# Attention, gated layer and softplus layer in one kernel: x left undivided by its rms in the first layer, and another form of the first batch's softmax

## The chip, the cores and the metric

The kernel runs on one core of a Trainium2 chip. The metric is device time in microseconds (us). TensorE does the matrix products into eight PSUM banks; VectorE and ScalarE read these banks and work on SBUF; GpSimd helps VectorE with work in SBUF; SyncE issues the transfers between HBM and SBUF. Each engine runs its own list of instructions in order and waits at semaphores for the others.

## The reference

Three stages run one after the other on 4 batches of 576 tokens.

```
scores = q @ k.T / 8           # 8 heads of 64; heads 0-3 local: the 32 latest keys,
                               # heads 4-7 strided: keys at the same position modulo 32
attn = exp(scores - max); attn = attn / (sum(attn) + 1e-9)
x = (attn @ v), laid out as 2304 tokens x 512
xn = x / sqrt(mean(x * x) + 1e-6) * rms_g          # one rms for each token
x = (silu(xn @ w_gate) * (xn @ w_val)) @ w_out     # 512 -> 1536 -> 512
h = x @ w_in; x = softplus(h) @ w_out2             # 512 -> 2048 -> 512
```

## The kernel before, in words

**Layout.** x stands turned, features on partitions, as four tiles of 128 features (kk = 0 to 3). The 2304 tokens are cut in chunks c of 512 (the last of 256). Side A is chunks 0 and 1 (side index 0), side B is chunks 2, 3 and 4. A float32 product is made of halves: each operand is split into a high half and a low half, and `mm3` (L434) issues three matmuls for each product. Splitting x takes a ScalarE copy (L351, tile `ob`) and a subtraction (L355 when it is on VectorE, L356 on GpSimd). Weights come in packed words, and `decode` (L370 to L376) unpacks them with one ScalarE and three VectorE instructions before they are split into `win` or `wout`.

**Attention.** A unit is one batch, one pair of heads and one half of its blocks. Local pairs have blocks of 64 queries and 96 keys, 5 and 4 of them in the two units; strided pairs have blocks of 54, 6 and 5 of them. Units 0 to 15 are batches 0 and 1 and run in `attend`, as the startup of the program; units 16 to 31 are put between the first layer's work by `steps`. A unit goes: mask and scores on TensorE (L553, L566), maximum on VectorE (L581), exponentials on ScalarE, sums and division (L610, L611, `stage_p`), transposes of the probabilities (L637), their eviction to `pt`, product with v (L660), eviction to `xs`. For units 0 to 15 the exponentials are one instruction for each block, straight from the bank and with the row's sum as a second result (L599); for units from 16 on VectorE subtracts the maximum first (L583), one ScalarE instruction does the whole unit (L596), and VectorE adds up (L609).

**Statistics and the first layer.** `stats(c)` squares the chunk on ScalarE (L452), sums over features by four matmuls with ones (L453), takes a logarithm and an exponential (L457, L458) and three VectorE steps (L459 to L462); `norm` then multiplies x by the result and by rms_g (L472), and only then is x split. `half(f, c)` makes the gate and value products of block f of 128 hidden features for chunk c; Gate and value banks of side A come from one ring of two. `chain1` takes silu of the gate bank (L867), multiplies by the value bank (L868) and splits (L856 and `gl` on L355); `out1` is the product with w_out, added into x by L899 and L901. The startup does blocks 0 and 1 for chunk 0, then `stats(1)` between two loads of ScalarE's function table, then `half(0, 1)`. After that `side_a` goes through the blocks for both chunks, with queued steps of attention in between. `gv` is a ring of buffers for chain1; the `ssq` rows of chunks 0 and 1 join it once these chunks are divided.

**Order.** Engine calls are recorded as nodes with a cost and their reads and writes (`Program.add`). `emit` plans the nodes of a whole section: it gives each a due time, tries several orders against a model of the engines (with LEAVE, SWITCH and the costs of DMAs), picks for some nodes VectorE or ScalarE, or VectorE or GpSimd (`evict`, `two`), and issues the best order found. So a change of a cost or of a dependency can move instructions anywhere in the section. One section runs from the start to block 9 of side A, a second one covers the rest.

Of the kernel before, what the change touches and what calls it, by code (L numbers as in the profile page):

```python
# [49 lines left out]
WINDOW = 3413  # L50
TURNS, KEEP, SWITCH, LEAVE = 8, 0.5, 125, 4000

# [195 lines left out]
def attn_glu_softplus(  # L248
# [16 lines left out]
    def all_of(key):  # L265
        return (key, 0, 1 << 30)
# [81 lines left out]
    def split_op(src, ksrc, slot, k, n0=0, eng="POOL"):  # L348
# [11 lines left out]

    hold = []

    def decode(src, t, kt, keep):

        raw, kraw = raws.next()
        u, ku = cvu.next()
        words = raw.bitcast(U32).rearrange("p (n two) -> p n two", two=2)
        wlo, whi = words[:, :, 0], words[:, :, 1]
        dma(512, lambda: nc.sync.dma_start(out=raw, in_=src), hold, [kraw])
# [9 lines left out]
        dma(256, lambda: nc.sync.dma_start(out=wk[keep], in_=t), [kt], [("wk", keep, keep + 1)])  # L379

# [59 lines left out]
    def stats(c, ring_):  # L440
# [37 lines left out]
    def attention(at, use):  # L478

        def whole(u):  # L480
            return u >= 16

        qks = ring(at, "qk", 3, [128, 2 * QW])
        mask = at.tile([128, MW], BF16, name="mask")
        dma(100, lambda: nc.sync.dma_start(out=mask, in_=masks), [], [all_of("mask")])
        vb = ring(at, "vb", 2, [128, 9, 128])
        eb = ring(at, "eb", EB, [128, 5 * LK])
        pp = ring(at, "pp", 2, [128, 6, 128])
        pt = ring(at, "pt", 4, [128, 3 * 128])
        sq = ring(at, "sq", 2, [128, 6 * SK])  # L490
        mz = ring(at, "mz", 8, [128, 2, 6])
# [41 lines left out]
        def stage_s(u):  # L533
# [48 lines left out]
            if whole(u):  # L582
                dve(n * nk, lambda: nc.vector.tensor_sub(ev, sv, m.unsqueeze(2).to_broadcast([128, n, nk])),  # L583
                    [kb_, km], [ke])
            else:
                dve(6, lambda: nc.vector.tensor_scalar(out=m, in0=m, scalar1=-SCALE, scalar2=None, op0=ALU.mult),
                    [km], [km])
            scored[u] = (e, ke, ev, z, kz, sv, kb_, m, km)

        def stage_e(u):  # L590
            b, p, t0, n = units[u]
            loc = p < 2
            nk = LK if loc else SK
            e, ke, ev, z, kz, sv, kb_, m, km = scored.pop(u)
            if whole(u):
# [28 lines left out]
        def stage_t(u):  # L624
# [8 lines left out]
            for a0 in range(0, n, 3):  # L633
                m = min(n, a0 + 3) - a0
                tp, ktp = use.t.next()
                for a in range(m):
                    pr.add("PE", 108, lambda a=a, a0=a0, tp=tp: nc.tensor.transpose(  # L637
                        tp[:kp, a * 128:a * 128 + 128], pv[:, a0 + a, :], id_sb), [kpv, all_of("id")], [ktp])
                t, kt = pt.next()
                evict(2 * m * nq, t[:kp, :2 * m * nq].rearrange("p (m c) -> p m c", c=nq),  # L640
                      tp[:kp, :m * 128].rearrange("p (m c) -> p m c", c=64)[:, :, :nq], [ktp], [kt])
                res.append((t, kt))
            trans[u] = res
            if p >= 2:
                trans[u - 1] = res

        def stage_v(u):
# [8 lines left out]
            for a in range(n):  # L656
                t, kt = pts[a // 3]
                for h in range(2):
                    o = (2 * (a % 3) + (h ^ (u % 2))) * nq
                    pr.add("PE", 59, lambda a=a, h=h, o=o, t=t: nc.tensor.matmul(  # L660
                        xb[64 * h:64 * h + 64, a * nq:(a + 1) * nq], lhsT=vt[r0:r1, v0 + a, 64 * h:64 * h + 64],
                        rhs=t[r0:r1, o:o + nq], start=True, stop=True), [all_of(kv), kt],
                        [kx], mode=1 if loc else 3)
            g = rg_sb[:, p:p + 1]
            if loc:
# [70 lines left out]
    def steps(at, after, ring_):  # L736
# [3 lines left out]
        def turn(us, cs):  # L740
# [118 lines left out]

    def chain1(gate, val, n=CH, r4=False, eng="POOL"):  # L860
# [117 lines left out]
    with tc.manual_schedule():  # L978
# [56 lines left out]
        def side_a(f, queue):  # L1035
# [4 lines left out]
            for c in (0, 1) if f > 1 else (1,):  # L1040
# [12 lines left out]
        with ExitStack() as c2:  # L1053
# [7 lines left out]
            for f in (0, 1):  # L1061
                g[f, 0] = chain1(*gates.pop((f, 0)))
            o_banks.t = f_banks.t
# [13 lines left out]
            for i in (0, 1):  # L1077
                fk["gv"].keys[len(fk["gv"].t)] = ("ssq", i * CH, i * CH + CH)
# [139 lines left out]
```

## Time and profile before

| what | value |
|---|---|
| time, median of three runs | 901.63 us (901.39 to 902.55) |
| the profiled execution | 900.52 us, span 898.7 us, mean granted clock 0.993 |
| TensorE busy | 882.7 us, 98% of the span |
| VectorE busy | 712.9 us, 79% |
| ScalarE busy | 486.1 us, 54% |
| GpSimd busy | 28.1 us, 26 instructions |
| share of the chain that ended last | TensorE 67%, VectorE 3% |

A busy time is what the engine's rows cover, and a matmul's row runs a little past the start of the next one; shares over the whole span mix a startup, in which the engines wait for each other, with hundreds of microseconds in which TensorE never stops.

### The profile page before, as it was taken

How to read it: one execution, taken by the hardware profiler on the slowest of the kernel's cores; microseconds unless marked ns; L12 is line 12 of the kernel's file. 1: busy time of each engine (PE TensorE's matmuls, PEld its weight loads, DVE VectorE, ACT ScalarE, POOL GpSimd, SP SyncE). 2: the span in 40 equal slices, each digit the busy share in tenths (PEclk: the TensorE clock that was granted, in tenths of full speed). 3: DMA queues.
4: the chain of work that ended last, by engine and by line, in shares of the span. 5: the costliest groups of instructions: out<-in, count | busy, mean ns of one | idle time of the engine just before them, and what ended most of it. 6: DMA issues, size and time to landing. Idle time of an engine off the chain costs nothing.

```text
span 898.7 us, 14075 instructions
## 1 busy us (share of the span) xinstructions
PE 882.7 (98%) x5320; PEld 725.7 (81%) x5320; DVE 712.9 (79%) x1349; ACT 486.1 (54%) x999; POOL 28.1 (3%) x26
## 2 busy tenths in 40 slices
PE   7899999999999999999999999999999999999998
PEld 6567777778777888888888888888888888888886
DVE  4988898998599995888988799877798456676644
ACT  5987664545364675444545567544474655434331
POOL 0000010200000000000100100000000000000000
PEclk7999999999999999999999999999999999999999
DMA  7874667363040443344553025321114111111003
GB/s 254 263 228 146 205 205 224 124 214 106 13 141 23 151 152 105 134 146 140 183 154 104 2 85 178 137 71 48 47 47 153 36 47 48 47 32 39 1 1 117
DMA packets 41858, 102.18 MB, mean 114 GB/s; under 512 B 4800, under 2 KB 5568, under 8 KB 41792
## 3 DMA queue, kind: packets, MB, share of 16 engines
q1 hardware_dynamic: 41792, 101.31, 35.5%
q8 instruction: 41, 0.67, 0.3%
q14 instruction: 25, 0.20, 0.1%
HBM read 78.74 MB, written 22.54 MB: 113 GB/s over the span
## 4 chain that ended last, share of the span: by engine, by line
PE 67%; DVE 3%; issue 0%
PE bank L434 67%; DVE xs L901 1%; DVE ob L355 0%; DVE tb L355 0%; DVE xs L355 0%; DVE win L355 0%; DVE w L355 0%; DVE ssq L355 0%; DVE glx L355 0%; DVE xs L919 0%; DVE gv L355 0%; DVE ssq L868 0%; DVE gv L868 0%; DVE gl L355 0%
## 5 line engine op out<-in xcount | busy, mean ns | idle before, releaser
L434 PE MATMUL bank<-ob,win 128*128 128x512 f32 (+1 forms) x1560 | 430.8, 360 | 2.7 <-ACT ob L351 1.8
L434 PEld LDWEIGHTS bank<-ob,win 128*128 128x128 f32 x1560 | 283.4, 188 | 55.0 <-ACT ob L351 2.2
L434 PE MATMUL bank<-tb,win 128*128 128x512 f32 x672 | 232.8, 392 | 0.0
L434 PEld LDWEIGHTS bank<-tb,win 128*128 128x128 f32 x672 | 125.4, 188 | 22.9 <-DVE xs L901 0.4
L919 DVE TENSOR_TENSOR xs<-bank,xs 128x512 f32<-128x512 f32 x126 | 86.8, 689 | 45.7 <-PE bank L434 44.4
L405 ACT ACTIVATE win<-w 128x512 fp32r<-128x512 f32 (+1 forms) x136 | 83.4, 616 | 63.9 <-PE bank L434 32.7
L355 DVE TENSOR_TENSOR win<-w,win 128x512 fp32r<-128x512 f32 (+1 forms) x134 | 89.5, 673 | 15.6 <-ACT win L405 12.6
L434 PE MATMUL bank<-wout,ghx 128*128 128x512 f32 x304 | 100.0, 390 | 0.0
L434 PE MATMUL bank<-wout,gh 128*128 128x512 f32 x272 | 90.4, 390 | 0.0
L434 PE MATMUL bank<-ghx,wout 128*128 128x512 f32 x224 | 84.1, 394 | 0.0
L434 PE MATMUL bank<-gh,wout 128*128 128x512 f32 (+1 forms) x256 | 81.3, 356 | 0.5 <-DVE xs L901 0.4
L901 DVE TENSOR_TENSOR xs<-bank,xs 128x512 f32<-128x512 f32 (+1 forms) x100 | 62.2, 628 | 8.9 <-PE bank L434 8.1
L434 PEld LDWEIGHTS bank<-wout,ghx 128*128 128x128 f32 x304 | 56.9, 188 | 11.7
L434 PEld LDWEIGHTS bank<-wout,gh 128*128 128x128 f32 x272 | 50.9, 188 | 10.6
L816 ACT ACTIVATE gv<-bank 128x512 f32<-128x512 f32 x48 | 28.4, 592 | 48.1 <-PE bank L434 47.6
L434 PE MATMUL bank<-wout,glx 128*128 128x512 f32 x152 | 53.2, 389 | 0.0
L434 PEld LDWEIGHTS bank<-gh,wout 128*128 128x128 f32 x256 | 45.5, 189 | 9.0 <-DVE xs L901 1.4
L434 PEld LDWEIGHTS bank<-ghx,wout 128*128 128x128 f32 x224 | 41.9, 188 | 8.4 <-ACT ghx L856 0.2
L434 PE MATMUL bank<-wout,gl 128*128 128x512 f32 x136 | 47.7, 389 | 0.0
L373 DVE SCALAR_TENSOR_TENSOR cvu<-raw,cvu 128x512 uint32<-128x512 uint32 x68 | 46.6, 686 | 1.0
L355 DVE TENSOR_TENSOR w<-w 128x256 f32<-128x256 f32 x109 | 45.4, 416 | 0.9
L820 DVE TENSOR_TENSOR gv<-bank,gv 128x512 f32<-128x512 f32 x48 | 32.9, 685 | 16.0 <-ACT gv L816 9.0
(131 smaller groups left out, 1211.8 us busy)
## 6 DMA issues: line engine op xcount, KB each, us to landing
raw<-w SPq DMA_DIRECT2D x68, 512.0 KB, 4.1
w<-w_kept SPq DMA_DIRECT2D x56, 256.0 KB, 2.6
w_kept<-cvtx SPq DMA_DIRECT2D x26, 256.0 KB, 3.7
cvt<-w_kept SPq DMA_DIRECT2D x26, 256.0 KB, 2.7
w_kept<-w SPq DMA_DIRECT2D x24, 256.0 KB, 4.2
qk<-qk SPq DMA_DIRECT2D x8, 601.0 KB, 5.6
w_kept<-cvt SPq DMA_DIRECT2D x18, 256.0 KB, 3.5
cvtx<-w_kept SPq DMA_DIRECT2D x18, 256.0 KB, 2.8
```

Of the source, the lines that this page charges most:

```text
L355: pr.add("DVE", 68 + n / 0.96, lambda: getattr(nc.vector, name)(o, x, y), r, w, alt=(110 + n * 2.3, lambda: getattr(nc.gpsimd, name)(o, x, ...
L373: dve(512, lambda: nc.vector.scalar_tensor_tensor(out=u, in0=wlo, scalar=29, in1=u, op0=ALU.logical_shift_right, op1=ALU.bitwise_or), [kra ...
L405: act(n, lambda: nc.scalar.activation(h, t, AF.Copy), [kt], [reg(0, o + lo, o + hi)])
L434: lambda a=a, b=b, i=i, st=st, mv=mv: nc.tensor.matmul(o, lhsT=st[a], rhs=mv[b], start=(first and i == 0), stop=(last and i == m - 1), ski ...
L816: act(CH, lambda: nc.scalar.activation(o, y[0], AF.Copy), [y[1]], [ko])
L820: dve(CH, lambda: nc.vector.tensor_add(o[0], y[0], o[0]), [y[1], o[1]], [o[1]])
L901: dve(n, lambda: nc.vector.tensor_add(x, pb, x), [kp, kx], [kx])
L919: dve(DM, lambda: nc.vector.tensor_add(x, pb, x), [kp, kx], [kx])
```

## The change

1. **Undivided x for side A** (`RAW`). x of chunks 0 and 1 is no longer multiplied by the statistics before it is split: `raw_op` splits x times rms_g (ScalarE copy with a scale, VectorE scalar_tensor_tensor). In `chain1` VectorE multiplies the gate bank by the statistics (new line L932) before silu, which now reads SBUF. The value product stays undivided, and at the end of side A x of chunks 0 and 1 is multiplied by the statistics once (eight `xs<-xs,ssq` pieces). As `ssq` is then needed all through side A, two new tiles `gvx` take its place in the ring of `gv`, and for blocks 10 and 11 the ring has two buffers.
2. **Statistics.** `stats(0)` is recorded after `half(0, 0)`. `stats(1)` loses its own pair of table loads: it runs in the first turn of `steps`, and five steps of the queue are recorded right after `half(0, 1)`.
3. **Batch 0's strided units** (2, 3, 6 and 7) use the form that units from 16 on have: subtraction, one exponential for the unit, sum on VectorE.
4. **Batch 0's first local pair** (units 0 and 1, `late`): VectorE subtracts, TensorE transposes the scores, and the exponential is the eviction of the transposed tile (L670). The product with v is turned round (queries on partitions) with a column of ones in v that gives the sums; VectorE divides (L685 to L689), and 18 small identity matmuls (L695) turn the result back.
5. **Planner numbers**: LEAVE 4000 to 6000, and other costs for some DMAs. v's tiles are 130 wide, not 128.

```diff
+RAW = (0, 1)
-TURNS, KEEP, SWITCH, LEAVE = 8, 0.5, 125, 4000
+TURNS, KEEP, SWITCH, LEAVE = 8, 0.5, 125, 6000
...
+    def raw_op(src, ksrc, slot, k, kk):
+        (h, l), (kh, kl) = op_of(slot, k)
+        g, kg = rg_sb[:, kk:kk + 1], all_of("rg")
+        act(CH, lambda: nc.scalar.activation(h, src, AF.Copy, scale=g), [ksrc, kg], [kh])
+        pr.add("DVE", 130 + CH / 0.96, lambda: nc.vector.scalar_tensor_tensor(
+            out=l, in0=src, scalar=g, in1=h.bitcast(F32), op0=ALU.mult, op1=ALU.subtract), [ksrc, kh, kg], [kl])
...
-        if c < 2:
+        if c < 2 and c not in RAW:
             norm(c, "DVE")
...
         def whole(u):
-            return u >= 16
+            return u >= 16 or u in (2,3,6,7)
+
+        def late(u):
+            return u in (0,1)
...
             else:
+                pv, kpv = ev, ke
...
+                dve(n * nk, lambda: nc.vector.tensor_sub(
+                    pv[:, :, :nk], sv, m.unsqueeze(2).to_broadcast([128, n, nk])), [kb_, km], [kpv])
...
+                if late(u):
+                    act(m * 128, lambda t=t, tp=tp, m=m: nc.scalar.activation(
+                        t[:kp, :m * 128], tp[:kp, :m * 128], AF.Exp, scale=SCALE), [ktp], [kt], True)
...
+        def turned(xb, kx, n, nq):
...
+            dve(6, lambda: nc.vector.tensor_scalar_add(out=z, in0=xv[:, :, 64], scalar1=1e-9), [kx], [kz])
+            dve(30, lambda: nc.vector.reciprocal(out=z, in_=z), [kz], [kz])
...
+            dve(n * 64, lambda: nc.vector.tensor_mul(
+                y, xv[:, :, :64], z.unsqueeze(2).to_broadcast([128, n, 64])), [kx, kz], [ky])
...
+                    pr.add("PE", 47, lambda a=a, r=r, i=i: nc.tensor.matmul(
+                        xt[r, a * nq:(a + 1) * nq], lhsT=y[i, a, :], rhs=id_sb[i, i], start=True, stop=True),
+                        [ky, all_of("id")], [kt], mode=3)
...
             for c in cs:
-                norm(c, "POOL")
+                if c > 1:
+                    norm(c, "POOL")
...
+        if c in RAW:
+            r, kr = sview(CUTS[c], CUTS[c + 1]), ("ssq", CUTS[c], CUTS[c + 1])
+            dve(n, lambda a=a, gb=gb: nc.vector.tensor_mul(a, gb, r), [kg, kr], [ka])
+            gb, kg = a, ka
         act(n, lambda: nc.scalar.activation(a, gb, AF.Silu), [kg], [ka], True)
...
         def early():
             use.s = s_banks
-            stats(0, f_banks)
             direct(0)
             half(0, 0, f_banks)
+            stats(0, v_banks)
...
-            table(EXP_LN)
-            stats(1, t_banks)
-            table("silu_and_others")
             direct(1)
             half(0, 1, v_banks)
...
-            queue, last_turn = steps(x, {1: (2,)}, tv)
+            queue, last_turn = steps(x, {-1: (1,), 1: (2,)}, tv)
+            step(queue, 5)
...
+        for c in RAW:
+            for kk in range(KD):
+                x, kx = xv(kk, c)
+                two("POOL", CH, "tensor_mul", x, x, sview(CUTS[c], CUTS[c + 1]), [kx, ("ssq", CUTS[c], CUTS[c + 1])], [kx])
+        give(RAW)
```

What stands on the engines is shown at three places. First ScalarE at the program's start, where `eb` is a unit's buffer of scores or probabilities. Before, from its first exponential on:

```order
L599 ACTIVATE eb_116,mz_129<-bank_71,mz_129 128x96
L599 ACTIVATE eb_115,mz_128<-bank_70,mz_128 128x96
L599 ACTIVATE eb_116,mz_129<-bank_71,mz_129 128x96
L599 ACTIVATE eb_115,mz_128<-bank_70,mz_128 128x96
L599 ACTIVATE eb_116,mz_129<-bank_71,mz_129 128x96
L599 ACTIVATE eb_115,mz_128<-bank_70,mz_128 128x96
L599 ACTIVATE eb_116,mz_129<-bank_71,mz_129 128x96
L599 ACTIVATE eb_115,mz_128<-bank_70,mz_128 128x96
L599 ACTIVATE eb_117,mz_130<-bank_76,mz_130 128x54
L599 ACTIVATE eb_115,mz_128<-bank_70,mz_128 128x96
```

And after the change:

```order
L625 ACTIVATE eb_119<-eb_119 128x270
L670 ACTIVATE pt_123<-bank_72 96x384
L670 ACTIVATE pt_124<-bank_73 96x256
L625 ACTIVATE eb_118<-eb_118 128x324
L670 ACTIVATE pt_125<-bank_72 96x384
L670 ACTIVATE pt_126<-bank_73 96x128
L283 ACTIVATE xs<-bank_75 128x320
L628 ACTIVATE eb_116,mz_136<-bank_71,mz_136 128x96
L628 ACTIVATE eb_120,mz_135<-bank_70,mz_135 128x96
L628 ACTIVATE eb_116,mz_136<-bank_71,mz_136 128x96
```

The exponentials by block of the first local pair (96 wide) and of the first strided pair (54 wide) are gone from there; in their place stand two whole exponentials of a strided pair and the exponentials of four transposed tiles (`pt`), and the first by block is that of another local pair.

Second VectorE where the first layer's first result is made, `gl` being the low half of the first hidden block of chunk 0 and `cvu`, `w` and `cvtx` the unpacking of weights. Before:

```order
L373 SCALAR_TENSOR_TENSOR cvu_81<-raw_78,cvu_81 128x512
L611 RECIPROCAL mz_135<-mz_135 128x5
L376 SCALAR_TENSOR_TENSOR w_82<-w_82,cvu_81 128x512
L355 TENSOR_TENSOR pp_121<-eb_115,mz_135 128x5x54
L355 TENSOR_TENSOR ssq_b<-ssq_b,sq_126 128x128
L868 TENSOR_TENSOR gv_84<-bank_76,gv_84 128x512
L355 TENSOR_TENSOR win_89<-w_82,win_89 128x512
L355 TENSOR_TENSOR gl_87<-gv_84,gh_85 128x512
L371 TENSOR_SCALAR cvu_81<-cvtx 128x512
L373 SCALAR_TENSOR_TENSOR cvu_81<-raw_79,cvu_81 128x512
L868 TENSOR_TENSOR gv_83<-bank_70,gv_83 128x512
```

And after the change:

```order
L471 SCALAR_TENSOR_TENSOR ssq<-gv_83,ssq 128x512
L364 TENSOR_TENSOR pp_122<-eb_116,mz_132 128x5x54
L932 TENSOR_TENSOR gv_84<-bank_76,ssq 128x512
L382 SCALAR_TENSOR_TENSOR cvu_81<-raw_79,cvu_81 128x512
L280 COPY pt_125<-bank_72 128x324
L935 TENSOR_TENSOR gv_84<-bank_77,gv_84 128x512
L932 TENSOR_TENSOR gv_83<-bank_71,ssq 128x512
L385 SCALAR_TENSOR_TENSOR cvtx<-cvtx,cvu_81 128x512
L364 TENSOR_TENSOR gl_87<-gv_84,gh_85 128x512
L281 TENSOR_SCALAR xs<-bank_74,rg_sb 128x128
L935 TENSOR_TENSOR gv_83<-bank_70,gv_83 128x512
```

Both gate banks (`bank_76` and `bank_71`) are now read by VectorE, with `ssq`, and the step L471 that makes `ssq` stands directly ahead of the first of them.

Third VectorE at the end of side A, where x of side A gets its last pieces (`xs<-bank`) and the operands of side B are built (`tb`, and `ob` from x). Before:

```order
L355 TENSOR_TENSOR tb<-gv_83,tb 128x512
L355 TENSOR_TENSOR xs<-xs,ssq_b 128x256
L355 TENSOR_TENSOR ob<-xs,ob 128x256
L355 TENSOR_TENSOR tb<-xs,tb 128x512
L355 TENSOR_TENSOR xs<-xs,ssq_b 128x256
L355 TENSOR_TENSOR ob<-xs,ob 128x256
L901 TENSOR_TENSOR xs<-bank_72,xs 128x512
L901 TENSOR_TENSOR xs<-bank_75,xs 128x512
L901 TENSOR_TENSOR xs<-bank_73,xs 128x512
L355 TENSOR_TENSOR ob<-xs,ob 128x256
L355 TENSOR_TENSOR ob<-xs,ob 128x512
```

And after the change:

```order
L364 TENSOR_TENSOR glx_103<-gv_83,ghx_100 128x512
L364 TENSOR_TENSOR xs<-xs,ssq_b 128x256 x2
L364 TENSOR_TENSOR tb<-xs,tb 128x512
L968 TENSOR_TENSOR xs<-bank_74,xs 128x512
L968 TENSOR_TENSOR xs<-bank_75,xs 128x512
L364 TENSOR_TENSOR xs<-xs,ssq 128x512 x2
L968 TENSOR_TENSOR xs<-bank_72,xs 128x512
L968 TENSOR_TENSOR xs<-bank_73,xs 128x512
L364 TENSOR_TENSOR xs<-xs,ssq 128x512 x2
L364 TENSOR_TENSOR xs<-xs,ssq_b 128x256
L364 TENSOR_TENSOR tb<-xs,tb 128x512
L364 TENSOR_TENSOR ob<-xs,ob 128x512
```

Four of the eight multiplications of x by `ssq` stand ahead of the `ob` pieces there, the other four some rows behind.

## Rows read from the trace of the kernel before

**Rows 1.** busy time by stretch; us, then busy us (instructions) of each engine, granted clock, DMA

```profile
0.00:10.00 10.00, 7.19 (x106) 6.23 (x107) 2.56 (x11) 2.76 (x10) 1.61 (x6) 1.00 0.80 252
10.00:30.00 20.00, 16.63 (x322) 13.60 (x321) 15.37 (x52) 16.81 (x99) 0.00 (x0) 0.74 0.83 284
30.00:62.00 32.00, 28.03 (x328) 19.43 (x329) 29.04 (x74) 28.89 (x109) 0.00 (x0) 1.00 0.73 228
62.00:80.00 18.00, 17.16 (x139) 11.49 (x138) 14.38 (x26) 14.98 (x26) 0.00 (x0) 1.00 0.54 171
80.00:220.00 140.00, 139.83 (x1113) 110.91 (x1112) 129.53 (x267) 80.64 (x140) 13.35 (x10) 1.00 0.56 174
220.00:270.00 50.00, 49.75 (x290) 39.45 (x289) 37.10 (x63) 24.77 (x44) 1.41 (x1) 1.00 0.31 96
270.00:300.00 30.00, 29.25 (x136) 23.34 (x135) 29.94 (x56) 14.39 (x27) 1.29 (x1) 1.00 0.13 36
300.00:600.00 300.00, 299.96 (x1509) 254.53 (x1508) 255.92 (x474) 167.96 (x304) 8.75 (x7) 1.00 0.40 128
```

**Rows 2.** timeline of TensorE; start, us, engine, line, operation, out<-in, count [idle before]

```profile
63.54 0.39 PE L434 MATMUL bank<-gh,wout 128*128 128x512 f32 x1
...
76.55 8.02 PE L434 MATMUL bank<-ob,win 128*128 128x512 f32 x34 [0.39 <-ACT ob L351]
```

**Rows 3.** timeline of ScalarE: exponentials by block, a table load, whole exponentials

```profile
8.52 0.34 ACT L599 ACTIVATE eb<-bank,mz 128x96 f32<-128x96 f32 x1 [6.51 <-DVE mz L586]
...
8.85 0.33 ACT L599 ACTIVATE eb<-bank,mz 128x96 f32<-128x96 f32 x1
...
13.06 0.39 ACT L599 ACTIVATE eb<-bank,mz 128x54 f32<-128x54 f32 x1
...
13.34 0.39 ACT L599 ACTIVATE eb<-bank,mz 128x54 f32<-128x54 f32 x1
...
73.05 1.28 ACT L291 ACT_TABLE_LOAD   x1
74.34 0.67 ACT L370 ACTIVATE w<-raw 128x512 f32<-128x512 f32 x1
...
86.90 0.79 ACT L596 ACTIVATE eb<-eb 128x324 f32<-128x324 f32 x2 [1.20 <-DVE eb L583]
```

**Rows 4.** timeline of VectorE, startup and the first whole units

```profile
7.22 1.12 DVE L581 TENSOR_REDUCE mz<-bank 128x4 f32<-128x384 f32 x2 [6.21 <-PE bank L566]
...
61.98 0.69 DVE L355 TENSOR_TENSOR gl<-gv,gh 128x512 fp32r<-128x512 f32 x1 [0.90 <-ACT gh L856]
...
74.75 2.08 DVE L472 SCALAR_TENSOR_TENSOR xs<-xs,rg_sb,ssq 128x512 f32<-128x512 f32 x3
...
85.64 0.83 DVE L581 TENSOR_REDUCE mz<-bank 128x6 f32<-128x324 f32 x2
86.39 0.83 DVE L583 TENSOR_TENSOR eb<-bank,mz 128x324 f32<-128x324 f32 x2
```

**Rows 5.** waits from 0 to 62 us; total us, times, longest

```profile
PE bank L553 <- ACT eb L599: 3.3, 2, 2.9
DVE mz L610 <- ACT eb L599: 2.0, 3, 1.0
...
DVE cvu L371 <- ACT w L370: 1.2, 1, 1.2
```

**Rows 6.** timeline of TensorE where the second side of layer 1 starts

```profile
285.70 0.50 PE L434 MATMUL bank<-gh,wout 128*128 128x512 f32 x1 [0.40 <-DVE xs L901]
...
290.11 1.19 PE L434 MATMUL bank<-ob,win 128*128 128x512 f32 x4 [0.24 <-DVE xs L901]
```

**Rows 7.** timeline of VectorE beside a GpSimd instruction

```profile
270.45 0.67 DVE L868 TENSOR_TENSOR gv<-bank,gv 128x512 f32<-128x512 f32 x1
271.05 1.51 DVE L355 TENSOR_TENSOR ob<-xs,ob 128x512 fp32r<-128x512 f32 x1
```

**Rows 8.** timeline of GpSimd there

```profile
270.71 1.29 POOL L356 TENSOR_TENSOR tb<-xs,tb 128x512 fp32r<-128x512 f32 x1 [12.16 <-PE bank L434]
```

More of the change, by code (lines that the diff above doesn't have):

```diff
@@ L378, in decode @@
             op0=ALU.logical_shift_left, op1=ALU.bitwise_or), [kt, ku], [kt])
-        dma(256, lambda: nc.sync.dma_start(out=wk[keep], in_=t), [kt], [("wk", keep, keep + 1)])
+        dma(170, lambda: nc.sync.dma_start(out=wk[keep], in_=t), [kt], [("wk", keep, keep + 1)])
     def fetch(t, kt, keep):
@@ L489, in attention @@
         pt = ring(at, "pt", 4, [128, 3 * 128])
+        gvx.update((i, at.tile([128, CH], F32, name=f"gvx{i}")) for i in RAW)
         sq = ring(at, "sq", 2, [128, 6 * SK])
@@ L526, in load_v @@
             vals[u // 2] = (vt, kv)
-            dma(nt * (48 if p < 2 else 50), lambda: nc.sync.dma_start(out=vt[:kp, :nt, :], in_=src), [], [all_of(kv)])
+            dma(nt * (31 if p < 2 else 41), lambda: nc.sync.dma_start(out=vt[:kp, :nt, :], in_=src), [], [all_of(kv)])
         def half(u, h):
@@ L584, in stage_s @@
                     [kb_, km], [ke])
-            else:
+            elif not late(u):
+                dve(6, lambda: nc.vector.tensor_scalar(out=m, in0=m, scalar1=-SCALE, scalar2=None, op0=ALU.mult),
+                    [km], [km])
+            else:
+                pv, kpv = ev, ke
+                if not loc:
+                    if t0 == 0:
+                        both[u // 2] = pp.next()
+                    pv, (kpv, _, _) = both[u // 2]
+                    o = 64 if t0 else 0
+                    pv, kpv = pv[:, :n, o:o + 64], (kpv, o, o + 64)
+                dve(n * nk, lambda: nc.vector.tensor_sub(
+                    pv[:, :, :nk], sv, m.unsqueeze(2).to_broadcast([128, n, nk])), [kb_, km], [kpv])
+                probs[u] = (pv, kpv)
                 dve(6, lambda: nc.vector.tensor_scalar(out=m, in0=m, scalar1=-SCALE, scalar2=None, op0=ALU.mult),
@@ L645, in stage_t @@
                 trans[u - 1] = res
+        def turned(xb, kx, n, nq):
+            xv = xb[:, :n * 65].rearrange("p (a c) -> p a c", c=65)
+            z, (kz, _, _) = mz.next()
+            z, kz = z[:, 1, :n], (kz, 0, 10)
+            dve(6, lambda: nc.vector.tensor_scalar_add(out=z, in0=xv[:, :, 64], scalar1=1e-9), [kx], [kz])
+            dve(30, lambda: nc.vector.reciprocal(out=z, in_=z), [kz], [kz])
+            y, ky = xq.next()
+            y = y[:, :n * 64].rearrange("p (a c) -> p a c", c=64)
+            dve(n * 64, lambda: nc.vector.tensor_mul(
+                y, xv[:, :, :64], z.unsqueeze(2).to_broadcast([128, n, 64])), [kx, kz], [ky])
+            xt, kt = use.v.next()
+            for a in range(n):
+                for h in range(2):
+                    r, i = slice(64 * h, 64 * h + 64), slice(64 * h, 64 * h + nq)
+                    pr.add("PE", 47, lambda a=a, r=r, i=i: nc.tensor.matmul(
+                        xt[r, a * nq:(a + 1) * nq], lhsT=y[i, a, :], rhs=id_sb[i, i], start=True, stop=True),
+                        [ky, all_of("id")], [kt], mode=3)
+            return xt, kt
         def stage_v(u):
@@ L658, in stage_v @@
                 for h in range(2):
+                    if late(u):
+                        o = (2 * (a % 3) + (h ^ (u % 2))) * 64
+                        pr.add("PE", 60 if loc else 40, lambda a=a, h=h, o=o, t=t, xb=xb: nc.tensor.matmul(
+                            xb[64 * h:64 * h + 64, a * 65:(a + 1) * 65], lhsT=t[r0:r1, o:o + 64],
+                            rhs=vt[r0:r1, v0 + a, 65 * h:65 * h + 65], start=True, stop=True), [all_of(kv), kt],
+                            [kx], mode=1 if loc else 3)
+                        continue
                     o = (2 * (a % 3) + (h ^ (u % 2))) * nq
-                    pr.add("PE", 59, lambda a=a, h=h, o=o, t=t: nc.tensor.matmul(
-                        xb[64 * h:64 * h + 64, a * nq:(a + 1) * nq], lhsT=vt[r0:r1, v0 + a, 64 * h:64 * h + 64],
+                    pr.add("PE", 59 if loc else 36, lambda a=a, h=h, o=o, t=t: nc.tensor.matmul(
+                        xb[64 * h:64 * h + 64, a * nq:(a + 1) * nq], lhsT=vt[r0:r1, v0 + a, 65 * h:65 * h + 64],
                         rhs=t[r0:r1, o:o + nq], start=True, stop=True), [all_of(kv), kt],
                         [kx], mode=1 if loc else 3)
+            if late(u):
+                xb, kx = turned(xb, kx, n, nq)
             g = rg_sb[:, p:p + 1]
@@ L991, in direct, with give @@
                 x, kx = xview(kk, CUTS[c], CUTS[c + 1])
+                if c in RAW:
+                    raw_op(x, kx, slots[kk // 2], kk % 2, kk)
+                    continue
                 split_op(x, kx, slots[kk // 2], kk % 2, eng="DVE" if kk % 2 or c and kk < 3 else "POOL")
         gates = {}
+        def give(cs):
+            for c in cs:
+                fk["gv"].keys[len(fk["gv"].t)] = ("ssq", c * CH, c * CH + CH)
+                fk["gv"].t.append(ssq[:, c * CH:c * CH + CH])
         def half(f, c, ring_):
@@ L1046, in side_a @@
                 step(queue)
-                g[f, c] = chain1(gate, val, eng="DVE" if f < DEALT else "POOL")
+                g[f, c] = chain1(gate, val, eng="DVE" if f < DEALT else "POOL", c=c)
                 drain(1 if f < W1N - 1 else 0)
@@ L1061, in attn_glu_softplus @@
             for f in (0, 1):
[L1062 removed]
+                g[f, 0] = chain1(*gates.pop((f, 0)), c=0)
             o_banks.t = f_banks.t
@@ L1086, in attn_glu_softplus @@
             pr.emit()
+            if RAW:
+                fk["gv"].t, fk["gv"].keys = fk["gv"].t[:2], {}
+                give(i for i in (0, 1) if i not in RAW)
         o_banks.t = banks.t[4:6] + banks.t[2:4]
@@ L1171, with ones @@
     vpad[:, :, 32:] = vt[:, :nloc]
-    vla = np.stack([vpad[:, :, 64 * i:64 * i + LK] for i in range(9)], axis=3)
+    def ones(x):
+        x = x.reshape(*x.shape[:-1], 2, D)
+        x = np.concatenate([x, np.ones_like(x[..., :1])], axis=-1)
+        return x.reshape(*x.shape[:-2], 2 * D + 2)
+    vla = ones(np.stack([vpad[:, :, 64 * i:64 * i + LK] for i in range(9)], axis=3))
     vst = np.zeros((B, nloc, 11 * SK, 128), np.float32)
@@ L1178 @@
     vsa[:, :, 64:64 + SK, :5] = vst[:, :, :, 6:]
+    vsa = ones(vsa)
     r = np.arange(64)[:, None]
```

22 lines of the change are left out of this document (16 added, 6 removed).

## The prediction

> **What bounds the kernel now.** I read the busy time by stretch first. TensorE has 299.96 us of rows in the 300 us after 300, and 139.83 of 140 between 80 and 220, while in the first 80 us it has 7.19 of 10, 16.63 of 20, 28.03 of 32 and 17.16 of 18, and between 270 and 300 it has 29.25 of 30 [rows 1]. So there are two places where a change of order can give time back: the startup with some 11 us of holes, and the seam between side A and side B with 0.75. Anywhere else a saving on VectorE or ScalarE is worth nothing, and a load on them costs only if TensorE runs dry.
>
> In the startup no engine is full. From 10 to 62 us VectorE has 44.4 of 52 and ScalarE 45.7 of 52, so they idle 7.6 and 6.3 us: they wait for one another and for TensorE. The waits up to 62 us say how: TensorE waits 3.3 us for banks that the exponentials by block still read (2.9 in one piece), VectorE 2.0 us for sums that come out of them, and 1.2 us for a copy that stood behind them on ScalarE [rows 5]. The milestone I use is the first `gl`, the last operand of the first `out1`, at 61.98 on VectorE [rows 4]; the first `out1` matmul follows at 63.54 [rows 2]. TensorE's instructions ahead of that matmul are of the same kinds and counts in both programs, but for 18 small transposes, another form of the 18 products with v that they belong to, and 12 more small products of strided units (78 instead of 66). So what the startup gains is what `gl` comes earlier. Behind it TensorE lacks 0.84 us of 18 up to 80, with the last wait, 0.39 us, at the start of `half(0, 1)` at 76.55 [rows 1, 2].
>
> **The change part by part.**
>
> *Exponentials of batch 0, ScalarE.* Two instructions by block start 0.33 us apart at 96 columns and 0.28 at 54 [rows 3]. 9 of the former and 22 of the latter go: 3.0 + 6.2 = 9.2 us. Four whole exponentials come, 0.79 us for two of 324 [rows 3], so about 1.5 for all four; the exponentials at the eviction take the place of copies of the same tiles, for nothing more. ScalarE loses about 7.7 us in the first 40, and the 2.9 us for which a bank stayed locked [rows 5], since a subtraction of 0.42 us frees it.
>
> *The same on VectorE.* Subtractions: 0.83 us for two of 324 [rows 4], and by width 0.35 for 270, 0.49 and 0.61 for the local pair: 2.6 us for six. Sums: the nearest row is the maximum over 324, two in 0.83 [rows 4]: 1.5 us for four. The division of the turned products, 320 and 256 wide, by the same rate 0.75.
>
> *Undivided x.* A 512-wide piece starts 0.60 us after the one before (270.45 to 271.05 [rows 7]). The 24 gates cost 24 x 0.60 = 14.4 us of VectorE, the eight multiplications at the end of side A 4.8. Eight instructions of L472 go, three in 2.08 us [rows 4], 0.69 each: 5.5 us. The new split (scalar_tensor_tensor) I put at 0.69 where the subtraction took 0.60: 0.7 more. Net 14.4 us more VectorE, nearly all after 62 us.
>
> *VectorE ahead of the first `gl`.* By the order: 2.6 + 1.5 + 0.75 from batch 0, two gates 1.2, the unpacking of one more weight tile 1.5; gone are four subtractions of `ob` (2.4; the four of L472 are replaced one for one), two divisions of `eb` (1.1), a weight's subtraction (0.6) and about 1.0 of small ones that went to ScalarE or GpSimd. Sum: 2.4 us more. So the gain can only be waiting. Of the 7.6 us that VectorE idles, all may stay (`gl` 2.4 us later) or all may go (5.2 earlier). I take 6.0: the 2.0, 1.2 and 0.9 us put down to ScalarE [rows 4, 5] and 1.9 of the rest, since TensorE's long wait behind it was for ScalarE too. The first 7 us, up to the first maximum [rows 4], are loading and stay. `gl` then comes 6.0 - 2.4 = 3.6 us earlier.
>
> *Statistics.* The four squares, the matmuls, the logarithm and the steps on VectorE stay and are only done later. `stats(0)` now ends directly ahead of the first gate, and queued behind this gate on VectorE are the first value product, `gl` and the split of chunk 1: if its four squares come late, these four are late. `stats(1)` no longer delays `half(0, 1)`: three of its four L472 end at 76.8 [rows 4], beside a TensorE that was nearly full, so what it gives back is at most the 0.84 us of holes. I take 0.8, and keep 0.
>
> *Table loads.* Two go. One took 1.28 us at 73.05, and the next copy started at 74.34, right behind it [rows 3]: 2.6 us of ScalarE for two, none of it at a place where TensorE waited. The Trainium skill (ScalarE: Activation LUTs, What ACT_TABLE_LOAD costs) counts a drain of about 1.38 us on top for every switch, an estimate of 5.3 us for the two. The row shows no gap for it here; by the page the sum would be the same, since ScalarE is not what is late there.
>
> *The 18 transposes* have no row. The nearest are the weights' matmuls, 34 in 8.02 us [rows 2], 0.24 for 512 columns; for 64 columns I take 0.06, 1.1 us in all, bounded by 0 and 4.3. They lie in the startup, where TensorE waits anyway. If that cover goes, they cost their 1.1.
>
> *The seam.* TensorE waits here 0.40 + 0.24 us for VectorE's pieces of x [rows 6]; VectorE is full from 270 to 300 (29.94 of 30 [rows 1]). Four multiplications, 2.4 us, now stand ahead of the last `ob`, but `stats(2)` and the last attention units come some five steps earlier. From 80 to 270 VectorE has 166.6 of 190 us [rows 1], so 23 free for 15. I take a doubling of the waits, 0.6 us, between -0.6 and 4.8.
>
> *GpSimd* gets nine more pieces (26 to 35 with the constants). One beside VectorE shows a price: the `ob` piece at 271.05 took 1.51 us, where its neighbour took 0.67, while GpSimd worked from 270.71 to 272.00 [rows 7, 8]. Nine times 0.84 is 7.6 us of VectorE, inside the 23 - 15 = 8 that are left, at nothing in the forecast. The Trainium skill (SBUF — State Buffer, Who interferes with whom) has a rule for this: a VectorE instruction with both inputs in SBUF and a GpSimd instruction that reads SBUF exclude each other for the whole instruction. The row agrees. By the rule each of the nine may stall VectorE for up to 1.29 us [rows 8], 11.6 in all, which is more than is left; that is part of the third rival.
>
> *LEAVE and the DMA costs* act only through the order, which is counted as it stands. v's 130 instead of 128 columns are 1.6% of a transfer, beside other loads.
>
> Sum: -3.6 - 0.8 + 0.6 = -3.8 us. From 900.5 us for the profiled execution that is 896.7; the median of the runs stands 1.1 above that execution, so **897.8 us**.
>
> **The rivals.**
>
> *More.* All of VectorE's idle time goes: 5.2 + 0.8 us, and the clock helps. Between 10 and 30 us TensorE was granted 0.74 of full speed, a mix of 1.2 and 2.4 GHz, after it had waited 2.9 us [rows 1, 5]. If it runs at 2.4 GHz there, up to 16.6 x 0.26 = 4.3 us of its rows shorten. Against it: the loads are busy 0.83 of that stretch. With all 10.3 us it would be 891.3; half of the clock's part gives 893.5.
>
> *Nothing.* VectorE takes ScalarE's place. Its work ahead of `gl` rises by 2.4; if only 3 of 7.6 us of idle time go, `gl` gains 0.6, the holes give 0.8, the seam takes 0.6: 0.8 us less, 900.8. For it: VectorE is already as full as ScalarE from 30 to 62 (29.0 to 28.9 of 32). Against it: the waits named above stand on the chain of ScalarE.
>
> *Slower: the gate banks wait for VectorE.* Before, ScalarE with 80.6 of 140 us freed a gate bank; now VectorE does, with 129.5 of 140 [rows 1], and TensorE may not start a next block's gate before. It decides once VectorE's free 23 us are used up, by the 15 more and the stalls beside GpSimd. If then each of the 20 gates of blocks 2 to 11 holds TensorE for half a piece, 20 x 0.3 = 6.0, and the four multiplications at the seam are paid in full, 2.4, the sum is -3.6 - 0.8 + 8.4 = +4.0: 905.6. Against it: the chain after 80 us is TensorE's, and the bank ring has two.
>
> *The change does not shorten the wait that it aims at*, since the qk loads come late: it ends as *Nothing*.
>
> **How the numbers follow.** A run of this kernel can tell about 0.2%, 1.8 us, from no change. The forecast (895 to 899.8) gets 0.47, *More* 0.2, *Nothing* in either form 0.17, *Slower* 0.16. Faster than 899.8: 0.47 + 0.2 + a little of *Nothing*, 0.68; within: 0.16; slower: 0.16. For 8 in 10 the range leaves out the far half of *More* and the far half of *Slower*: from 892.0 to 904.5. The forecast's own range is 895 to 900.
>
> **What would show it.** In the changed profile: no long wait of TensorE for exponentials near 12 us; the first `out1` matmul at about 60 us, not 63.5; no hole in TensorE at the start of `half(0, 1)`; VectorE above 93% from 80 to 270. The startup step is wrong if the first `out1` comes at 62 or later, and the seam's if TensorE waits there more than 2 us. Waits of TensorE for L932 between 80 and 270 would make the prediction wrong towards slower.

## The result, and the profile after

The changed kernel takes 912.53 us (904.24 to 914.39, four runs) against 901.51 us beside it: 1.0118 times as long, 95% interval [1.0071, 1.0165]. In a second measurement (`again`, below) it took 908.65 us, 1.0113 [1.0084, 1.0141]. The prediction, 897.8 us in a range from 892.0 to 904.5, is wrong, and on the wrong side.

The profiled execution is the quickest of the four: 904.24 us at a mean granted clock of 0.998, where the other three had 0.991 to 0.994 and took 911 to 914. So its rows show 3.7 us of loss (the profile before is one of 900.52), not the whole 11. By stretch, in the columns of [rows 1]:

```profile
0.00:10.00 10.00, 7.37 (x111) 6.31 (x112) 3.29 (x10) 1.28 (x1) 1.62 (x6) 1.00 0.80 245
10.00:30.00 20.00, 16.21 (x424) 13.79 (x424) 19.22 (x64) 17.58 (x70) 0.73 (x1) 0.99 1.00 342
30.00:62.00 32.00, 29.20 (x295) 21.27 (x294) 26.89 (x68) 27.32 (x96) 2.42 (x2) 0.95 0.69 224
62.00:80.00 18.00, 18.00 (x125) 13.14 (x124) 14.81 (x28) 13.05 (x24) 0.00 (x0) 1.00 0.73 209
80.00:220.00 140.00, 135.68 (x1119) 106.58 (x1118) 132.92 (x272) 78.13 (x139) 10.88 (x9) 1.00 0.53 167
270.00:300.00 30.00, 29.02 (x137) 23.24 (x136) 30.00 (x56) 14.13 (x27) 7.26 (x5) 1.00 0.09 26
```

Up to 80 us it goes as forecast: TensorE is full from 62 on (18.00 of 18), and by 80 us it has issued 84 of the first layer's gate and value matmuls, where the kernel before had issued 63 (the other kinds are level, and the transposes of L695 come on top):

```profile
L443 PE MATMUL bank<-ob,win 128*128 128x512 f32 x84 | 25.6, 437 | 0.2 <-ACT win L414 0.2
```

and before:

```profile
L434 PE MATMUL bank<-ob,win 128*128 128x512 f32 x63 | 16.4, 405 | 2.4 <-ACT ob L351 1.8 <-ACT win L405 0.5
```

At 0.24 us each the 21 are 5.0 us ahead, by estimate. So behind 80 us this execution loses nearly 9 us; 4.7 of them show as more idle time of TensorE, most of it between 80 and 220, where TensorE has 135.68 us of 140 and had 139.83 [rows 1]. The timeline of TensorE at the first `out1` matmul, at its three longest holes from there to 300 us (1.75, 1.47 and 0.74) and at one that stands behind L932:

```profile
60.41 0.73 PE L443 MATMUL bank<-gh,wout 128*128 128x512 f32 x2
...
86.55 0.72 PE L666 MATMUL bank<-id_sb,eb 128*96 128x128 f32 x5 [1.75 <-DVE eb L364]
...
114.97 3.25 PE L443 MATMUL bank<-ob,win 128*128 128x512 f32 x13 [0.64 <-DVE gv L932]
...
162.65 5.51 PE L443 MATMUL bank<-ob,win 128*128 128x512 f32 x23 [1.47 <-DVE gv L935]
...
272.49 0.72 PE L443 MATMUL bank<-gh,wout 128*128 128x512 f32 x2 [0.18 <-DVE xs L968]
...
274.19 0.73 PE L443 MATMUL bank<-gh,wout 128*128 128x512 f32 x2 [0.74 <-DVE xs L968]
```

The first `out1` came at 60.41, 3.1 us earlier than in [rows 2]. Each hole has VectorE named. VectorE at the first `gl`, and ahead of the three holes:

```profile
59.70 0.68 DVE L364 TENSOR_TENSOR gl<-gv,gh 128x512 fp32r<-128x512 f32 x1
...
83.46 1.26 DVE L639 TENSOR_SCALAR mz<-mz 128x5 f32<-128x5 f32 x1
...
85.76 0.65 DVE L364 TENSOR_TENSOR eb<-eb,mz 128x480 f32<-128x480 f32 x1
...
159.89 0.16 DVE L639 TENSOR_SCALAR mz<-mz 128x6 f32<-128x6 f32 x1
...
161.16 0.64 DVE L639 TENSOR_SCALAR mz<-mz 128x5 f32<-128x5 f32 x1
161.91 0.69 DVE L935 TENSOR_TENSOR gv<-bank,gv 128x512 f32<-128x512 f32 x1
...
272.36 1.17 DVE L364 TENSOR_TENSOR gv<-xs,gv 128x512 f32<-128x512 f32 x1
273.46 1.27 DVE L968 TENSOR_TENSOR xs<-bank,xs 128x512 f32<-128x512 f32 x2
```

`gl` started at 59.70, where it was 61.98 [rows 4]. An addition to five or six sums a partition (L639) takes 0.16 us at 159.89 and 1.26 at 83.46; the `eb` that TensorE waits for is queued behind it. GpSimd's timeline shows what stood beside it:

```profile
83.32 1.38 POOL L365 TENSOR_TENSOR win<-w,win 128x512 fp32r<-128x512 f32 x1 [31.57 <-PE bank L443]
...
160.01 1.76 POOL L365 TENSOR_TENSOR wout<-cvt,wout 128x512 fp32r<-128x512 f32 x1 [14.76 <-DVE mz L638]
...
267.08 5.90 POOL L365 TENSOR_TENSOR ob<-xs,ob 128x512 fp32r<-128x512 f32 x1 [6.35 <-ACT ob L353]
```

The two long L639 end with GpSimd's pieces, at 84.70 and 161.77. In the other direction, `ob` at 267.08 took GpSimd 5.90 us, up to 272.98, and the row of VectorE at 272.36 beside its end took 1.17 us, where 512 columns usually take it 0.67. These are the stalls of [rows 7, 8], this time on TensorE's path at all three holes. Last, ScalarE's waits for DMAs from 80 to 500 us (total, times, longest):

```profile
ACT cvtx L379 <- DMA w_kept<-cvtx: 9.4, 6, 4.7
...
ACT win L414 <- DMA w<-w_kept: 7.9, 6, 3.0
...
ACT w L379 <- DMA raw<-w: 6.7, 7, 1.5
...
ACT cvt L379 <- DMA raw<-w: 5.6, 5, 1.6
...
ACT wout L434 <- DMA cvt<-w_kept: 4.8, 2, 3.8
...
ACT cvtx L379 <- DMA raw<-w: 2.7, 3, 1.1
...
ACT cvt L379 <- DMA w_kept<-w: 0.4, 1, 0.4
```

They sum to 37.5 us. In the kernel before the same sum is 13.5.

### The profile page after: what moved, and what is told of

The parts are those of the page before. It is cut to its first block, busy times and chain, and to the rows that moved or that the text cites. A ratio compares the mean times of both kernels' runs of the same rounds, so it can differ in the third digit from the quotient of the medians.

```text
span 902.5 us, 14133 instructions
## 1 busy us (share of the span) xinstructions
PE 883.4 (98%) x5356; PEld 726.3 (80%) x5356; DVE 723.1 (80%) x1366; ACT 475.6 (53%) x943; POOL 43.5 (5%) x35
## 4 chain that ended last, share of the span: by engine, by line
PE 77%; DVE 12%; DMA 5%; ACT 4%; issue 1%; DVEq 0%; ACTq 0%; SPq 0%
PE bank L443 72%; DMA raw<-w 3%; DMA w_kept<-cvtx 2%; DVE cvu L382 1%; DVE xs L968 1%; PE bank L666 1%; PE bank L720 1%; DVE win L364 1%; PE bank L580 1%; DMA w<-w_kept 1%; ACT eb L628 1%; ACT xs L283 1%; DVE cvu L380 1%; DVE mz L595 1%; DVE gv L364 0%
## 5 line engine op out<-in xcount | busy, mean ns | idle before, releaser
L443 PE MATMUL bank<-ob,win 128*128 128x512 f32 (+1 forms) x1560 | 441.9, 362 | 2.4 <-DVE gv L935 1.5
L443 PE MATMUL bank<-tb,win 128*128 128x512 f32 x672 | 236.8, 394 | 0.3 <-DVE gv L883 0.2
L364 DVE TENSOR_TENSOR win<-w,win 128x512 fp32r<-128x512 f32 (+1 forms) x126 | 83.7, 666 | 18.2 <-ACT win L414 15.4
L443 PEld LDWEIGHTS bank<-gh,wout 128*128 128x128 f32 x256 | 45.1, 189 | 10.2 <-DVE xs L968 2.5
L443 PE MATMUL bank<-glx,wout 128*128 128x512 f32 x112 | 43.5, 395 | 0.0
```

Of the source, the lines that this page charges most:

```text
L443: lambda a=a, b=b, i=i, st=st, mv=mv: nc.tensor.matmul(o, lhsT=st[a], rhs=mv[b], start=(first and i == 0), stop=(last and i == m - 1), ski ...
```

## The experiments

All but the first three edit the planner's numbers or a part of the change. "Idle" is 420 us less TensorE's busy time from 80 to 500 us in the profiled execution, "DMA waits" the sum of ScalarE's waits as above. "Old" DMA costs are those of before. Both sums are of one execution: in `after` (904.24) and `dma_only` (906.35) it is 8 and 5 us faster than the median beside it in the table.

| kernel | operations | LEAVE | DMA costs | us | ratio [95%] | idle | DMA waits |
|---|---|---|---|---|---|---|---|
| before | before | 4000 | old | 900.8 to 901.5 | 1 | 1.2 | 14 |
| after | changed | 6000 | new | 912.53 | 1.0118 [1.0071, 1.0165] | 5.7 | 38 |
| again | changed | 6000 | new | 908.65 | 1.0113 [1.0084, 1.0141] | 9.5 | 47 |
| nogate | changed, gate multiplications left out | 6000 | new | 909.66 | 1.0107 [1.0084, 1.0131] | 4.8 | 35 |
| soft | softmax only | 6000 | new | 914.17 | 1.0159 [1.0131, 1.0186] | 5.9 | 34 |
| raw | undivided x only | 6000 | new | 906.97 | 1.0071 [1.0059, 1.0083] | 4.6 | 53 |
| leave4 | changed | 4000 | new | 904.34 | 1.0051 [1.0032, 1.0069] | 4.3 | 37 |
| dma_old | changed | 6000 | old | 907.62 | 1.0082 [1.0064, 1.0100] | 4.6 | 10 |
| old_numbers | changed | 4000 | old | 901.33 | 1.0007 [0.9997, 1.0017] | 1.6 | 8 |
| dma_high | changed | 4000 | higher | 911.48 | 1.0116 [1.0094, 1.0139] | 3.4 | 1 |
| numbers_only | before | 6000 | new | 911.00 | 1.0126 [1.0104, 1.0148] | 6.8 | 39 |
| dma_only | before | 4000 | new | 911.26 | 1.0104 [1.0080, 1.0128] | 3.5 | 35 |
| dma_decode | before | 4000 | weights' new | 903.37 | 1.0033 [1.0017, 1.0048] | 3.7 | 33 |
| dma_attn | before | 4000 | others' new | 903.25 | 1.0022 [1.0013, 1.0032] | 2.3 | 13 |
| leave_only | before | 6000 | old | 904.24 | 1.0032 [1.0019, 1.0045] | 0.9 | 15 |
| null4100 | before | 4100 | old | 903.69 | 1.0028 [1.0013, 1.0043] | 2.5 | 12 |
| null520 | before | 4000 | one at 520 | 902.36 | 1.0013 [1.0002, 1.0025] | 2.2 | 12 |
| raw_old | undivided x only | 4000 | old | 898.33 | 0.9971 [0.9959, 0.9983] | 1.7 | 12 |
| raw_whole | raw_old + whole units | 4000 | old | 901.73 | 1.0008 [0.9994, 1.0023] | 1.5 | 13 |
| raw_late | raw_old + late pair | 4000 | old | 903.62 | 1.0024 [1.0010, 1.0038] | 2.5 | 9 |

**First round: which part, and is it the clock?** `again` has no edit. The others:

```diff
 soft: statistics, division, give() and steps() as before, and
-RAW = (0, 1)
+RAW = ()
 raw:
-            return u >= 16 or u in (2,3,6,7)
+            return u >= 16
-            return u in (0,1)
+            return False
 leave4:
-TURNS, KEEP, SWITCH, LEAVE = 8, 0.5, 125, 6000
+TURNS, KEEP, SWITCH, LEAVE = 8, 0.5, 125, 4000
```

> The changed kernel once more, to see where its time lies in an execution at its median. Theory V (VectorE): the 24 gate multiplications make TensorE wait in side A, and that alone is the loss: the time spreads because the waits do; 904 to 914 us, the clock granted in full after 60 us. Rival C (clock): the waits are the smaller part; after one of them TensorE's granted clock falls to 1.2 GHz for some 10 us in a stretch in which TensorE is the bound, in most executions but not in all; 904 where it does not, 911 to 914 where it does, and the profile's clock column shows it in side A.

> The changed softmax of batch 0 alone (late local pair, whole strided pairs, LEAVE 6000); x is divided by its rms before the split as before, with stats(0) and stats(1) at their old places. No gate multiplications. Theory V and rival C: both expect no waits of TensorE between 80 and 270 us above 0.5 us, and 897 to 901 us, the startup's gain kept. Rival S (the softmax form itself costs, through its subtractions on VectorE): 903 us or more.

> The undivided x and the shared statistics turn alone; all of batches 0 and 1 keeps the exponentials by block. Theory V and rival C: the waits for L932 and L935 between 80 and 270 us stay, the startup gains little; 903 to 914 us. Rival S: 901 us or less.

> The changed kernel with LEAVE at 4000 as before. If the planner's number is the cause (it keeps TensorE longer in one kind of work, and so lets a late operand stop it), the waits in side A shrink and it comes to 901 us or less; theory V and rival C expect 903 to 914 us, since the same multiplications stand on VectorE.

`again` was granted the full clock throughout (1.0) and took 908.56 in that execution: the clock is not needed for a loss of 8 us, rival C falls as the main cause. Against theory V stands `soft`: no gate multiplications, and the slowest of all, 914.17, a clear miss. Rival S falls by `raw`: without the new softmax the loss is still 6 us (906.97). `leave4`, 904.34, lies at the low end of what V and C expected, but 4.3 us below `again` on the same operations. What all these share is the new DMA costs, and but for `leave4` the new LEAVE: the planner's numbers, which I had listed as the fifth part of the change and priced at nothing.

**Second round: the planner's numbers.**

```diff
 numbers_only (on the kernel before; old_numbers: both reversed on the changed kernel;
 dma_old: only the DMA costs reversed there)
-LEAVE = 4000
+LEAVE = 6000
-dma(512, ... out=raw ...)   dma(256, ... out=wk[keep] ...)
+dma(340, ... out=raw ...)   dma(170, ... out=wk[keep] ...)
-dma(nt * (48 if p < 2 else 50), ...)   mask 100, identity 64
+dma(nt * (31 if p < 2 else 41), ...)   mask 140, identity 40
 nogate:
-            dve(n, lambda a=a, gb=gb: nc.vector.tensor_mul(a, gb, r), [kg, kr], [ka])
-            gb, kg = a, ka
```

> The kernel before with nothing but the changed planner numbers (LEAVE 6000 and the lower costs of the DMAs that load packed weights, keep unpacked ones and load v). Theory P (planner numbers): they alone make the order worse, mostly in side B of layer 1 after 300 us, where ScalarE then waits for fetched weights; 904 to 912 us. Rival V (VectorE's new work is the loss): 899 to 902 us, no difference.

> The changed kernel with all planner numbers of before: the operations of the change with LEAVE 4000 and the old DMA costs. Theory P: most of the loss goes, 896 to 900 us. Rival V: the gate multiplications still stop TensorE in side A, 902 to 906 us.

> The changed kernel with the old DMA costs and LEAVE 6000. Theory P: TensorE's losses after 300 us fall back from 5 to 7 us to about 3, and 901 to 906 us in all; rival V expects 906 to 910 us, as the changed kernel.

> The changed kernel without the 24 multiplications of the gate banks by the statistics: this part of the computation is left out, silu reads the bank. VectorE has 14.4 us less to do before 290 us. Rival V: TensorE's losses between 80 and 300 us fall from 20 to 22 us to about 14 as before, 900 to 903 us. Theory P: the order's other faults stay, 904 us or more.

This settles what the loss hangs on. Not one operation is changed in `numbers_only`, and it takes 911.0 us; `old_numbers` has all the changed operations and takes 901.33, no different from before. `nogate` leaves out the 24 multiplications (VectorE has 712.3 us of rows in it, 723.1 in the changed kernel) and gains nothing over 908.65. From 80 to 500 us, first `numbers_only`:

```profile
80.00:500.00 420.00, 413.22 (x2539) 339.18 (x2539) 355.65 (x680) 219.63 (x393) 26.78 (x21) 1.00 0.44 137
```

then `old_numbers`:

```profile
80.00:500.00 420.00, 418.40 (x2590) 344.49 (x2589) 379.63 (x716) 225.02 (x403) 29.62 (x25) 1.00 0.44 140
```

and `nogate`:

```profile
80.00:500.00 420.00, 415.17 (x2564) 339.47 (x2563) 359.94 (x686) 220.90 (x395) 24.30 (x19) 1.00 0.45 140
```

TensorE is busy 413.22, 418.40 and 415.17 of 420; VectorE has 355.65 in the first, where TensorE loses most, so the loss does not follow VectorE's load. Theory P held in the sum, but not in its place: `numbers_only` lost 5.9 of its 6.8 us of idle time before 300 us, not in side B, `old_numbers` missed the gain that P expected, and `dma_old`, 907.62, came out above P's 901 to 906, where V had expected it.

**Third round: which number, and in which direction?**

```diff
 leave_only, dma_only: one of the two edits of numbers_only, on the kernel before
 raw_old: raw with both numbers old
 dma_high (on old_numbers): packed weights 512 -> 600, keep 256 -> 500, fetch 256 -> 300
```

> The kernel before with LEAVE 6000 alone. Of the 10.2 us that both planner numbers cost on it: if LEAVE costs what it cost on the changed kernel (907.6 against 901.3, 6.3 us), 905 to 909 us, with more loss of TensorE between 80 and 300 us and ScalarE's waits for DMAs at about 13 us as before. Rival: the two only hurt together, 902 or less.

> The kernel before with the changed DMA costs alone. If they act as on the changed kernel (904.3 against 901.3, 3.0 us), 902.5 to 906 us, and ScalarE's waits for DMAs between 80 and 500 us go from 13 to 35 us or more. Rival: the two only hurt together, 902 or less.

> The changed operations with LEAVE 4000 and DMA costs above the old ones, set by the times to landing (packed weights 512 to 600, keeping unpacked ones 256 to 500, fetching them 256 to 300 in the planner's unit). If too low a cost is what hurts, a cost near the landing times does no harm and may help: 896 to 901.5 us, ScalarE's waits for DMAs between 80 and 500 us at 8 us or less. Rival (any other number than the tuned one makes the order worse): 903 us or more.

> The undivided x and the shared statistics turn alone, with the old planner numbers. If the operations of the change cancel out (old_numbers: 901.3), this part with its 14 us more VectorE is the harmful one: 902 to 906 us; rival: it is the part that gains, since it takes x's division out of the startup: 896 to 900 us.

On the kernel before, the DMA costs alone do all of it (911.26), LEAVE only 3 us; both miss their expectations, the one above, the other below. On the changed operations it is the other way round: over `old_numbers` LEAVE costs 6.3 us (`dma_old`) and the DMA costs 3.0 (`leave4`). So a number has no price of its own. Costs set higher, with hardly a wait of ScalarE for a DMA left (1.3 us), cost as much (911.48), so a loss of this size needs neither too low a cost nor these waits. `raw_old` is the one version faster than the kernel before; its expectation had called that the rival.

**Fourth round: what does any new order cost?**

```diff
 null4100, null520 (on before): LEAVE 4000 -> 4100; packed weights 512 -> 520
 raw_whole, raw_late (on raw_old): only u in (2,3,6,7) whole; only u in (0,1) late
 dma_decode, dma_attn (on before): only raw 340 and keep 170; only v, mask and identity
```

> The kernel before with LEAVE 4100 instead of 4000: a change too small to mean anything, but the order written is another one from row 91 of ScalarE on. Theory N (numbers: lower DMA costs and a higher LEAVE are wrong in themselves): 900 to 902.5 us. Rival O (the order of before is a lucky one of many, and any new order costs): 903 us or more.

> The kernel before with the cost of a packed weight's load at 520 instead of 512, again too small to mean anything, with another order from row 73 of ScalarE on. Theory N: 900 to 902.5 us, ScalarE's waits for DMAs between 80 and 500 us near 13 us. Rival O: 903 us or more.

> Old planner numbers, undivided x and the shared statistics turn, and batch 0's strided units with one exponential each; the first local pair keeps its exponentials by block. raw_old without the whole units came to 898.3, with them and the late pair 901.3 (old_numbers). If the late pair (subtractions, turned product) is what costs those 3 us, 896 to 899 us; if the whole units are, 900 to 903 us; rival O: either, or more.

> Old planner numbers, undivided x and the shared statistics turn, and the first local pair in its late form; batch 0's strided units keep their exponentials by block. If the late pair costs the 3 us between 898.3 and 901.3, 900 to 903 us; if the whole units do, 896 to 899 us; rival O: either, or more.

> The kernel before with only two of the DMA costs changed: packed weights 340 instead of 512, keeping unpacked ones 170 instead of 256. Theory D (the weights' costs are what hurts: ScalarE's copies are put in the list ahead of their data and hold up what stands behind): ScalarE's waits for DMAs between 80 and 500 us at 30 us or more, 905 to 912 us. Rival A (the costs of the attention's loads, which set the startup, are what hurts): waits near 13 us, 900 to 903.5 us.

> The kernel before with only the other DMA costs changed: v's tiles 31 and 41 instead of 48 and 50 per block, the mask 140 instead of 100, the identity 40 instead of 64. Theory D: 900 to 903.5 us, in the scatter that a new order has (null4100, null520). Rival A: 905 us or more, TensorE losing in the first 80 us.

Numbers that mean nothing give 1.0028 and 1.0013: the order before is better than the two neighbours tried, by 1 to 3 us. `null4100` is what rival O expected, `null520` what theory N did. `dma_decode` refutes theory D: the 33 us of ScalarE's waits are there and the time is 903.37. `dma_attn`, 903.25, refutes rival A. Neither half of the DMA costs leaves this scatter by more than the intervals, both together cost 10 us. `raw_whole` and `raw_late` are both slower than `raw_old`, by 3.4 and 5.3 us; the one is hardly more than the scatter, the other up to twice it, and both parts together (`old_numbers`) cost 3.0, so neither part has the loss to itself.

Over the whole table the two kinds do not overlap: the eight rows with all the new DMA costs take 904.3 to 914.2 us, the seven with the old ones (or one at 520) and LEAVE at 4000 or 4100 take 898.3 to 903.7.

## Why the prediction was wrong

*The step that failed* is the sentence "LEAVE and the DMA costs act only through the order, which is counted as it stands". It was priced at nothing, and no rival had it. It is the whole loss: +10.2 us on unchanged operations (`numbers_only`), and without it the change is 0.07% slower, which is no difference (`old_numbers`). I had read the order at three places and taken the rest as good; the two longest holes came elsewhere, at 86.55 and 162.65.

*The startup* was right for this order: `gl` forecast at 58.4, measured at 59.70 (59.91 in `again`); TensorE full from 62 on; about 5.0 us ahead by 80 us, where 3.6 and 0.8 had been forecast. But it too hung on the order. With the same operations and the old numbers the first `out1` matmul comes later than before:

```profile
66.46 0.39 PE L443 MATMUL bank<-gh,wout 128*128 128x512 f32 x1
```

So the 3.6 us do not belong to the operations as such, and the 7.7 us taken from ScalarE are not a gain that every order keeps.

*The 24 gates and "Slower"*: this rival gave 905.6 and the right sign for the wrong reason. Two holes stand at gate or value products (1.47 us behind L935, 0.64 behind L932, a sign that the prediction had named), but without the gate multiplications the time stays at 909.66. Nor was VectorE as full as the other sign wanted: 90% from 80 to 270 us, not above 93%.

*GpSimd's pieces* were counted, nine more at nothing, but it is their place that matters. Between 80 and 220 us there are fewer of them than before (9 for 10), and yet two stand on TensorE's path there; the third hole has `ob` at the seam. The rows that they lengthen are 1.10, 0.48 and 0.50 us over their usual time, 2.1 of the 4.0 us of the three holes if all of it passes on. How much of the loss they are was not tried alone.

*The seam* was forecast at 1.24 us of waits and had 0.92, in two pieces (0.18 and 0.74); in `again` it had 1.7.

*What stays open*: why the new numbers make a worse order, and why the DMA costs together cost 10 us on the kernel before and each half 2 to 3. No single wait carries it. In the profiled execution of `numbers_only`, 10.1 us longer than that of before, TensorE's idle time is 8.1 us more (24.2 for 16.1): 2.2 of it in the first 80 us, 5.6 from 80 to 500. The other 2.0 are rows of TensorE that took longer in sum (884.6 for 882.7). In this table all kernels with the weights' new DMA costs, or higher ones, idle 3.4 us or more from 80 to 500, and those with the old costs and LEAVE near 4000 at most 2.5, but the idle time does not rank the times. Whether `raw_old` gains by its operations or by a lucky order is open too, since its 2.9 us are the size of the scatter. As it stands it is faster than both kernels.

## What to carry to other kernels

Where a planner writes the order, its numbers are an edit like any other: run them alone on the old operations, and the new operations with the old numbers, before any reason is looked for in an engine's load. Measure first what a number that means nothing does to the time (here 1 to 3 us, in two tries); a gain of that size cannot be credited to an operation. And a forecast made of three places in an order of thousands of rows needs a term for the rest.

## What the hardware showed

A short VectorE instruction can stand behind GpSimd: 0.16 us became 1.26 beside a piece of GpSimd that ended at the same time, on the chain to TensorE's longest hole (1.27 beside the same piece in `again`). The Trainium skill (SBUF — State Buffer, Who interferes with whom) names `tensor_scalar` among the operations that can take the port shared with GpSimd, where the one that starts first holds it for its whole instruction; the two rows at 83.46 and 161.16 agree, and show that five elements a partition are enough for it. In the other direction a GpSimd piece of 512 columns, 1.29 us in [rows 8], took 5.90 beside a VectorE that was never idle (30.00 of 30 us); which of VectorE's rows held it up is not shown, and in `again` the same piece took 2.89.

And after a hole TensorE can run at the lower of its two clocks, 1.2 GHz, in the midst of layer 1. In `dma_high`, TensorE's timeline behind a wait of 2.54 us:

```profile
277.35 0.53 PE L443 MATMUL bank<-ghx,wout 128*128 128x512 f32 x1 [2.54 <-DVE xs L968]
...
279.38 0.63 PE L443 MATMUL bank<-ghx,wout 128*128 128x512 f32 x1
279.81 0.63 PE L443 MATMUL bank<-gh,wout 128*128 128x512 f32 x1
...
281.57 0.62 PE L443 MATMUL bank<-gh,wout 128*128 128x512 f32 x2
```

From 279.38 to 279.81 one matmul of 512 columns takes 0.43 us, where [rows 2] have 0.24 each. The stretches around it, with the granted clock as the third number from the end:

```profile
270.00:277.00 7.00, 4.81 (x22) 3.65 (x20) 7.00 (x13) 5.28 (x11) 0.66 (x1) 1.00 0.55 183
277.00:282.00 5.00, 4.65 (x13) 3.68 (x14) 4.04 (x8) 3.17 (x6) 2.08 (x2) 0.66 0.00 0
282.00:290.00 8.00, 8.00 (x37) 6.60 (x36) 7.79 (x14) 3.46 (x7) 0.34 (x1) 1.00 0.40 131
```

TensorE was busy 4.81 of the 7 us ahead of 277. The clock is 0.66 from 277 to 282, a mix of 1.2 and 2.4 GHz, and full on both sides.
